# Making sixteen low weight halves on TensorE instead of VectorE, in an attention and two-layer-MLP kernel

## The chip, the cores and the metric

The kernel runs on one core of a Trainium2 chip, in one launch. The metric is the device time of that launch in microseconds (us). Before the change it is 1087.44 us, the median of three runs (1085.36 to 1089.29).

## The reference

Three layers follow each other, all in float32:

```
scores = q @ k^T / 8 + min(-(cum_i - cum_j), 0), causal      # cum = cumsum(max(s, 0))
x = softmax(scores) @ v                                      # 4 batches, 8 heads, 576 tokens, 64 wide
xn = x / rms(x) * rms_g                                      # 2304 tokens, 512 wide
x2 = (silu(xn @ w_gate) * (xn @ w_val)) @ w_out              # inner width 1536
out = (h - tanh(h)) @ w_out2,   h = x2 @ w_in                # inner width 2048
```

All weights arrive as float64 words. The kernel turns them into float32 and then into pairs of float16: a high half `hi = fp16(w * scale)` and a low half `lo = fp16(w * scale - hi)`. A product is three float16 matmuls (`mm3`, L675 to L678: high by high, high by low, low by high).

## The kernel before, in words

The work is tiled into 20 attention tiles of up to 128 query tokens (five to a batch) and six MLP blocks of 384 tokens. A block of the first MLP (`moe1_groups`: twelve `up1_g`/`up1_v` pairs, four `down1`) can start when its three or four attention tiles have been normalised (`emit_norm`, L513 to L531: ScalarE writes the high half of x, VectorE the low half at L529, two DMAs transpose them). A generator gives out the attention work in small steps, and the main program interleaves these with weight tasks and with MLP groups. The first block is interleaved with the preparation of the weights, the later ones with attention alone. A scheduler then sets each engine's own instruction order when the program is built; on the chip each engine works through its list in that order.

The weights of the first MLP are 24 pieces of 128 x 512 (`w1_tasks`): for j = 0, 1, 2 four gate pieces and four value pieces. A piece goes through these steps:

- a DMA brings its raw words into a part of tile `WO` (`raw_slots(WO, 2 * (n % 6))`, six places that are used in turn, issued at L540);
- VectorE decodes them in three instructions into float32 (L542 to L544, `w<-wo`), in `W1[:, n + 1, :]`;
- ScalarE squares the piece (L573) and TensorE adds up the squares (L589, `mm<-wo,rg`); a place for raw words is free again after that;
- after four pieces VectorE works out the scale (L593, L119 to L123, L596), a column of 128 numbers for each piece, `gsg` or `gsv`;
- `conv` calls `split`: ScalarE writes the high half (L558), VectorE the low half (L559), both into `W1[:, n, :]`. That is the place where the float32 of piece n - 1 lay, so the high half of a piece waits until the piece before has been read for the last time.

The weights of `w_out` (L559 `wo<-wo,tau`) and of the second MLP go through the same `split`. The names in the profile: `w` is the weight tile, `wo` the raw words or tile `WO`, `mm` a PSUM bank of the MLP, `st` the scores, `pv` the product with v, `sm` one of two PSUM banks (pool `ps_sm`) that the row maxima and small sums take in turn, `r` the row maxima, `tm`, `sh` and `sl` the MLP's inner values, `xth` and `xtl` the normalised x. In batch 0 the attention's product with v is in float32 (L477, 120 matmuls in the program, each of which the profile shows as two, with a weight load each), in the later batches in float16 (L479 to L481).

Of the kernel before, what the change touches and what calls it, by code (L numbers as in the profile page):

```python
# [7 lines left out]
FP32 = mybir.dt.float32  # L8
FP16 = mybir.dt.float16
# [31 lines left out]
def tile_forget_attention_moe_moe2(ctx, tc, qa, qb, kt, va, vb, va0, vb0, s, wg, wv, wo, rg, win, wo2, out):  # L41
# [28 lines left out]
    V, A, G, P, SY = nc.vector, nc.scalar, nc.gpsimd, nc.tensor, nc.sync  # L70

    ident = const.tile([128, 128], FP16, name="ident")
    bigid = const.tile([128, 128], FP16, name="bigid")
    maskn = const.tile([128, 128], FP16, name="maskn")
    ones_f = const.tile([128, 128], FP32, name="ones_f")
# [59 lines left out]
    def emit_consts():  # L135
        V.memset(lnp, LN_P)
        A.activation(out=warm, in_=lnp, func=ACTF.Exp)
        V.memset(halves, 0.0)
        for r in range(2):
            V.memset(halves[64 * r:64 * r + 64, r:r + 1], 1.0)  # L140
        V.memset(ident, 1.0)
        V.memset(bigid, 65504.0)
        V.memset(maskn, 0.0)
        V.memset(ones_f, 1.0)
        V.memset(ones_b, 1.0)
        V.memset(pat, 1.0)
        V.memset(pat[0:2], 0.0)
        G.affine_select(out=ident, in_=ident, pattern=[[1, 128]], compare_op=ALU.is_equal, fill=0.0, base=0, channel_multiplier=-1)
        G.affine_select(out=bigid, in_=bigid, pattern=[[1, 128]], compare_op=ALU.is_equal, fill=0.0, base=0, channel_multiplier=-1)
        G.affine_select(out=maskn, in_=maskn, pattern=[[-1, 128]], compare_op=ALU.is_ge, fill=-65504.0, base=0, channel_multiplier=1)  # L150
        for i in range(2):
            kc_consts(i)
        G.memset(tri, 0.0)
        G.affine_select(out=tri[:, 384:512], in_=tri[:, 384:512], pattern=[[-1, 128]], compare_op=ALU.is_ge, fill=-1e30, base=0, channel_multiplier=1)
        G.memset(spare(KC[2], 0)[0:64].bitcast(FP32), 0.0)
        for i in range(2):
            G.memset(QC[i][0:64].bitcast(FP32), 0.0)
        for i in range(2):
            G.memset(VT[i][64:128, 16:20, :].bitcast(FP32), 0.0)
# [396 lines left out]
    def split(W, n, sc):  # L556
        src, hi, lo = slot_f(W, n), slot_h(W, n), slot_l(W, n)
        A.activation(out=hi, in_=src, func=ACTF.Copy, scale=sc)  # L558
        V.scalar_tensor_tensor(out=lo, in0=src, scalar=sc, in1=hi, op0=ALU.mult, op1=ALU.subtract)  # L559

    def raw_tile(p, bufs):
        return p.tile([128, 512, 2], I32, name="raw", tag="raw", bufs=bufs)

# [14 lines left out]
    def w1_tasks(p):  # L578
# [24 lines left out]
                G.tensor_scalar(out=sig_s[j], in0=tl[j, "sg"], scalar1=sg, scalar2=2.0 ** -24, op0=ALU.mult, op1=ALU.mult)  # L603

        def conv(key, j, n, k):
            split(W1, n, tl[key, j, "s"][:, k:k + 1])

        for j in range(3):
            for key, src in (("g", wg), ("v", wv)):
# [584 lines left out]
```

## Time and profile before

| | us |
|---|---|
| median of three runs | 1087.44 |
| the profiled execution | 1086.19 |
| its span in the profile | 1084.4 |
| TensorE (PE) busy | 993.0 (92%) |
| VectorE (DVE) busy | 621.8 (57%) |
| ScalarE (ACT) busy | 604.1 (56%) |
| GpSimd (POOL) busy | 281.9 (26%) |

The profile's page divides the span into 40 slices. In the first eight (some 217 us) DVE is at 90% or more in most, while PE's slices lie between 10% and 90%; after them PE is at 90% or more nearly everywhere. Shares over the whole span therefore say little here: the stretch from 40 to 220 us is where weights are prepared beside attention, and it has to be read by itself.

### The profile page before, as it was taken

What the parts mean: (1) busy time and instruction counts of PE and PEld (TensorE: products, weight loads), DVE (VectorE), ACT (ScalarE), POOL (GpSimd) and SP (SyncE); (2) the same over time, 40 slices, a digit from 0 to 9 for tenths busy, and PEclk for the clock granted to TensorE, in tenths of its full rate; (3) what the DMA queues carried; (4) which work ended last, traced back from release to release, by engine and by line L of the source; (5) the groups of instructions that cost most, each with busy time, mean ns of one, the idle gap of its engine ahead of it and who ended that gap; (6) DMA issues with size and microseconds to landing.
All of it is one profiled execution on the core that took longest, in us unless ns stands there. A gap on an engine that the chain in (4) does not pass through costs nothing.

```text
span 1084.4 us, 19355 instructions
## 1 busy us (share of the span) xinstructions
PE 993.0 (92%) x7576; PEld 631.0 (58%) x7576; DVE 621.8 (57%) x1421; ACT 604.1 (56%) x1176; POOL 281.9 (26%) x377
## 2 busy tenths in 40 slices
PE   1488878899889999899999899999999999999998
PEld 1377545465556666556566556666666666666665
DVE  8987998966573540674543878485341605234250
ACT  6587668785854662767566447365342515243240
POOL 5122356424652450745345102100000000000000
PEclk9976989899999999999999999999999999999999
DMA  8714333330101212110100960141010010100000
GB/s 268 271 36 110 143 108 113 97 118 21 40 22 50 59 21 82 32 26 22 47 19 11 329 205 1 52 163 45 15 37 24 1 51 8 44 15 8 23 1 30
DMA packets 47517, 75.04 MB, mean 69 GB/s; under 512 B 25506, under 2 KB 33282, under 8 KB 46914
## 3 DMA queue, kind: packets, MB, share of 16 engines
q1 hardware_dynamic: 47426, 73.81, 21.5%
q8 instruction: 59, 0.97, 0.4%
q14 instruction: 32, 0.26, 0.1%
HBM read 59.42 MB, written 9.55 MB: 64 GB/s over the span
## 4 chain that ended last, share of the span: by engine, by line
PE 70%; DVE 15%; ACT 4%; DMA 4%; issue 4%; POOL 3%; SPq 0%; ACTq 0%; DVEq 0%; POOLq 0%
PE m L676 13%; PE m L678 13%; PE m L677 13%; PE mm L676 7%; PE mm L678 7%; PE mm L677 7%; PE pv L477 2%; PE st L435 1%; DVE w L559 1%; PE st L436 1%; POOL phl L457 1%; DVE w L543 1%; DVE q L351 1%; DMA w<-wo 1%; PE pv L479 1%
## 5 line engine op out<-in xcount | busy, mean ns | idle before, releaser
L676 PE MATMUL mm<-xth,w 128*128 128x384 f16 x480 | 160.9, 335 | 15.3 <-DVE tm L694 8.3
L678 PE MATMUL mm<-xth,w 128*128 128x384 f16 x480 | 159.9, 334 | 1.2 <-DVE w L559 1.2
L677 PE MATMUL mm<-xtl,w 128*128 128x384 f16 x480 | 160.7, 335 | 0.0
L1109 DVE SCALAR_TENSOR_TENSOR t<-m,u,t 128x384 f32<-128x384 f32 x96 | 59.2, 616 | 140.3 <-ACT t L1108 138.0
L677 PEld LDWEIGHTS <-w 128*128 128x128 f16 x960 | 95.0, 99 | 76.2 <-issue 22.8
L678 PEld LDWEIGHTS <-w 128*128 128x128 f16 x960 | 94.8, 99 | 65.2 <-issue 3.5
L676 PEld LDWEIGHTS <-w 128*128 128x128 f16 x960 | 95.8, 100 | 59.9 <-issue 4.4
L678 PE MATMUL m<-x2h,wi 128*128 128x384 f16 x384 | 125.2, 326 | 0.0
L677 PE MATMUL m<-x2l,wi 128*128 128x384 f16 x384 | 125.2, 326 | 0.0
L676 PE MATMUL m<-x2h,wi 128*128 128x384 f16 x384 | 125.2, 326 | 0.0
L678 PE MATMUL m<-dh,w 128*128 128x384 f16 x384 | 125.2, 326 | 0.0
L677 PE MATMUL m<-dl,w 128*128 128x384 f16 x384 | 125.2, 326 | 0.0
L676 PE MATMUL m<-dh,w 128*128 128x384 f16 x384 | 125.2, 326 | 0.0
L457 POOL TENSOR_TENSOR phl<-pf,phl 128x512 f16<-128x512 f32 (+2 forms) x90 | 96.0, 1073 | 46.6 <-ACT phl L450 45.7
L1116 POOL TENSOR_SCALAR io<-iso,isd 128x1 f32<-128x1 f32 x24 | 6.5, 271 | 375.8 <-ACT t L1122 314.4
L705 POOL TENSOR_TENSOR sl<-tm,sh 128x384 f16<-128x384 f32 x72 | 75.0, 1042 | 103.9 <-ACT sh L704 102.2
L445 POOL TENSOR_SCALAR_AFFINE_SELECT pf<-pf 128x128 f32<-128x128 f32 (+3 forms) x105 | 46.5, 445 | 187.2 <-ACT pf L443 186.8
L1110 ACT ACTIVATE dh<-t,sd 128x384 f16<-128x384 f32 x96 | 59.0, 615 | 60.9 <-DVE t L1109 60.7
L1122 ACT ACTIVATE t<-m,io 128x384 f32<-128x384 f32 x24 | 13.9, 580 | 141.0 <-PE m L678 141.0
L1111 DVE SCALAR_TENSOR_TENSOR dl<-t,sd,dh 128x384 f16<-128x384 f32 x96 | 59.2, 616 | 52.7 <-ACT dh L1110 51.9
L443 ACT ACTIVATE pf<-st,lnp,ilam 128x512 f32<-128x512 f32 (+2 forms) x105 | 73.1, 701 | 28.6 <-PE st L436 22.7
L676 PE MATMUL mm<-sh,wo 128*128 128x384 f16 x240 | 77.9, 326 | 1.8 <-DVE tm L694 1.8
(312 smaller groups left out, 2298.8 us busy)
## 6 DMA issues: line engine op xcount, KB each, us to landing
raw<-wo SPq DMA_DIRECT2D x16, 512.0 KB
w<-win SPq DMA_DIRECT2D x16, 512.0 KB
wo<-wg SPq DMA_DIRECT2D x12, 512.0 KB
wo<-wv SPq DMA_DIRECT2D x12, 512.0 KB
stk<-kt SPq DMA_DIRECT2D x4, 1152.0 KB
x2d<-tm SPq DMA_DIRECT2D x24, 192.0 KB
x2f<-x2d SPq DMA_DIRECT2D x6, 768.0 KB
out<-t SPq DMA_DIRECT2D x24, 192.0 KB
```

The lines of the kernel that those rows point to most:

```text
L443: A.activation(out=pf[:, 0:o], in_=ps[:, 0:o], func=ACTF.Exp, scale=bstate[b]["ilam"][:, hh:hh + 1], bias=lnp)
L445: G.affine_select(out=dg, in_=dg, pattern=[[0, len(heads)], [1, w]], compare_op=ALU.is_ge, fill=0.0, base=0, channel_multiplier=-1)
L457: G.tensor_tensor(out=u["pl"][:, 0:n], in0=u["pf"][:, 0:n], in1=u["ph"][:, 0:n], op=ALU.subtract)
L477: P.matmul(out=ps[0:w, o:o + 65], lhsT=u["pf"][:, cs], rhs=vs.bitcast(FP32), start=(c == 0), stop=(c == nch - 1))
L676: P.matmul(out=ps, lhsT=wh, rhs=xh, start=first, stop=False)
L677: P.matmul(out=ps, lhsT=wh, rhs=xl, start=False, stop=False)
L678: P.matmul(out=ps, lhsT=wl, rhs=xh, start=False, stop=last)
L705: moe_pend.append(lambda: G.tensor_tensor(out=SH["l"][:, f, :], in0=t, in1=SH["h"][:, f, :], op=ALU.subtract))
L1109: V.scalar_tensor_tensor(out=t, in0=ps, scalar=u[:, f // 4:f // 4 + 1], in1=t, op0=ALU.mult, op1=ALU.subtract)
L1110: A.activation(out=DH[:, f, :], in_=t, func=ACTF.Copy, scale=sd)
L1111: moe_pend.append(lambda: V.scalar_tensor_tensor(out=DL[:, f, :], in0=t, scalar=sd, in1=DH[:, f, :], op0=ALU.mult, op1=ALU.subtract))
L1122: A.activation(out=t, in_=ps, func=ACTF.Copy, scale=io)
```

## The change

For the pieces with j = 0 and 1, sixteen in all, `conv` calls a new function `split_pe`. It makes the low half by two matmuls into one `sm` bank: the float32 piece times a float32 diagonal of its scales, minus the high half through a float16 diagonal of -1. ScalarE makes the diagonal (128 x 128, from the identity) and brings the difference from PSUM to float16. The eight pieces of j = 2, and all other weights, stay with `split`. The diagonals lie in slot 12 of `WO`, one place for each k.

```diff
+    negid = const.tile([128, 128], FP16, name="negid")
...
+        V.memset(negid, -1.0)
...
+        G.affine_select(out=negid, in_=negid, pattern=[[1, 128]], compare_op=ALU.is_equal, fill=0.0, base=0, channel_multiplier=-1)
...
+    def split_pe(W, n, sc, i):
+
+        src, hi, lo = slot_f(W, n), slot_h(W, n), slot_l(W, n)
+        dg = WO[:, 12, 256 * i:256 * i + 256].bitcast(FP32)
+        A.activation(out=dg, in_=ident, func=ACTF.Copy, scale=sc)
+        A.activation(out=hi, in_=src, func=ACTF.Copy, scale=sc)
+        ps = sm_tile()
+        P.matmul(out=ps, lhsT=dg, rhs=src, start=True, stop=False)
+        P.matmul(out=ps, lhsT=negid, rhs=hi, start=False, stop=True)
+        A.activation(out=lo, in_=ps, func=ACTF.Copy)
+
...
         def conv(key, j, n, k):
-            split(W1, n, tl[key, j, "s"][:, k:k + 1])
+            if j < 2:
+                split_pe(W1, n, tl[key, j, "s"][:, k:k + 1], k)
+            else:
+                split(W1, n, tl[key, j, "s"][:, k:k + 1])
```

The scheduler orders every engine anew. Lines of the changed kernel are three higher than before from L151 to L560 (L529 becomes L532, L400 becomes L403, L542 becomes L545) and up to seventeen higher after (L676 becomes L693, L593 becomes L607, L589 becomes L603).

VectorE just ahead of the low half of tile 1's x (the second L529) before the change; `qke` to `qks` is the chain of batch 1's scales:

```order
L119 TENSOR_SCALAR qke<-sm 128x4
L120 TENSOR_SCALAR qke<-qke 128x4
L121 TENSOR_SCALAR qke<-qke 128x4
L123 RECIPROCAL qks<-qke 128x4
L246 TENSOR_SCALAR cap<-qke,sig_c 128x2
L593 TENSOR_REDUCE nmv_800<-mm 128x1
L247 TENSOR_TENSOR qks<-qks,cap 128x2
L386 TENSOR_REDUCE r8b<-sm 128x4
L529 SCALAR_TENSOR_TENSOR xl<-x,ss,xh 128x512
```

The same place after the change, up to the first step of the value pieces' scale:

```order
L545 TENSOR_SCALAR w_117<-wo 128x512 x2
L530 SCALAR_TENSOR_TENSOR ss<-ss 128x1
L546 SCALAR_TENSOR_TENSOR w_117<-wo,w_117 128x512 x2
L547 SCALAR_TENSOR_TENSOR w_117<-wo,w_117 128x512 x2
L245 TENSOR_SCALAR ssqk<-halves,ssqk 128x2
L532 SCALAR_TENSOR_TENSOR xl<-x,ss,xh 128x512
L499 SCALAR_TENSOR_TENSOR rr<-pv,vone 128x4
L500 RECIPROCAL rr<-rr 128x4
L607 TENSOR_REDUCE nmv_819<-mm 128x1
```

The normalisation of tile 1 now stands ahead of batch 1's scales and of tile 4's row maxima (L386); 20 rows earlier in VectorE's list (row 154, was 174), and that of tile 2 in row 179 (was 210).

TensorE where the first MLP block begins, after the change (L571 and L572 are the two new matmuls; L693 to L695 are `mm3`):

```order
L693 MATMUL mm<-xth,w_117 128x384
L694 LDWEIGHTS w_117
L694 MATMUL mm<-xtl,w_117 128x384
L695 LDWEIGHTS w_117
L695 MATMUL mm<-xth,w_117 128x384
L572 LDWEIGHTS negid
L572 MATMUL sm<-w_117,negid 128x512
L693 LDWEIGHTS w_117
L693 MATMUL mm<-xth,w_117 128x384
L571 MATMUL sm<-w_117,wo 128x512
L694 LDWEIGHTS w_117
L694 MATMUL mm<-xtl,w_117 128x384
```

The new matmuls stand between those of the MLP. In TensorE's list the first `mm3` matmul follows 58 of batch 0's 120 products with v where it followed 76, and seven L571 stand ahead of it; the twelfth `mm3` matmul follows eight L571. The last L571 stands ahead of the last ten of those 120.

ScalarE at the first gate pieces, before (`gsg` is the scale column):

```order
L416 ACTIVATE rt<-sm 16x128
L558 ACTIVATE w_116<-w_116,gsg_544 128x512 x2
L443 ACTIVATE pf<-st,lnp,ilam 128x512
L443 ACTIVATE phl<-st,lnp,ilam 128x512
L558 ACTIVATE w_116<-w_116,gsg_544 128x512 x2
L573 ACTIVATE wo<-w_116 128x512
L443 ACTIVATE pf<-st,lnp,ilam 128x512
```

And after (L568 makes a diagonal, L569 the high half):

```order
L419 ACTIVATE rt<-sm 16x128
L568 ACTIVATE wo<-ident,gsg_547 128x128
L569 ACTIVATE w_117<-w_117,gsg_547 128x512
L568 ACTIVATE wo<-ident,gsg_547 128x128 x3
L446 ACTIVATE pf<-st,lnp,ilam 128x512
L446 ACTIVATE phl<-st,lnp,ilam 128x512
L587 ACTIVATE wo<-w_117 128x512
```

Three of the four high halves have gone to later places, behind the exponentials of tile 1, and four diagonals have come in.

## Rows read from the trace of the kernel before

**Rows 1.** Busy time by stretch (us, instructions), TensorE's granted clock (1.00 is full), DMA.
```profile
core 0: us, PE busy (x) PEld busy (x) DVE busy (x) ACT busy (x) POOL busy (x), PEclk, DMA share, GB/s
40.00:100.00 60.00, 50.22 (x377) 42.18 (x376) 54.16 (x142) 45.85 (x92) 14.31 (x27) 0.75 0.33 88
100.00:160.00 60.00, 49.31 (x415) 30.89 (x413) 53.51 (x117) 38.35 (x82) 22.33 (x26) 0.87 0.39 122
160.00:220.00 60.00, 50.87 (x489) 32.29 (x488) 57.03 (x152) 46.88 (x104) 34.65 (x42) 0.90 0.34 104
220.00:240.00 20.00, 20.00 (x147) 12.38 (x146) 13.30 (x35) 17.13 (x37) 3.86 (x7) 1.00 0.47 142
```

**Rows 2.** The chain of waits, 40 to 160 us: shares, then pieces (start, us).
```profile
by line: PE pv L477 19.7%; DVE w L559 7.1%; issue 6.0%; DVE w L543 5.1%; DVE r L400 4.9%; DVE w L542 3.9%; DMA wo<-wv 3.7%; DVE w L544 3.7%; DMA wo<-wg 3.3%; DVE xl L529 2.7%; DVE kl L276 2.2%; PE st L435 2.2%; PE st L436 2.1%; PE mm L676 1
...
88.66 8.73 PE pv L477 x40
```

**Rows 3.** Busy time in 4 us stretches around 88 us, columns as in rows 1.
```profile
84.00:88.00 4.00, 0.77 (x11) 0.47 (x8) 4.00 (x12) 3.96 (x10) 2.74 (x3) 0.81 1.29 252
...
92.00:96.00 4.00, 4.00 (x21) 4.00 (x20) 3.22 (x12) 3.93 (x7) 1.36 (x3) 0.50 0.07 15
```

**Rows 4.** Timeline of TensorE: start, us, [idle before].
```profile
49.23 1.06 PE L477 MATMUL pv<-vt,pf 128*128 128x65 f32 x8
50.12 1.09 PE L477 MATMUL pv<-vt,phl 128*128 128x65 f32 x8
...
88.39 0.27 PE L414 MATMUL sm<-ident,r 128*8 128x128 f16 x1 [3.40 <-DVE r L411]
88.59 1.97 PE L477 MATMUL pv<-vt,pf 128*128 128x65 f32 x8
90.35 1.91 PE L477 MATMUL pv<-vt,phl 128*128 128x65 f32 x8
...
103.93 0.51 PE L676 MATMUL mm<-xth,w 128*128 128x384 f16 x1
104.23 1.91 PE L589 MATMUL mm<-wo,rg 128*128 128x512 bf16 x4
105.94 0.52 PE L677 MATMUL mm<-xtl,w 128*128 128x384 f16 x1
...
123.48 0.80 PE L477 MATMUL pv<-vt,phl 128*64 128x65 f32 x10
124.21 0.20 PE L435 MATMUL st<-q,kl 128*128 128x64 f16 x1
```

**Rows 5.** Groups of instructions, 40 to 160 us: count, busy us, mean ns, idle before.
```profile
L559 DVE SCALAR_TENSOR_TENSOR w<-w,gsg 128x512 f16<-128x512 f32 x8 | 8.6, 1070 | 0.0
L559 DVE SCALAR_TENSOR_TENSOR w<-w,gsv 128x512 f16<-128x512 f32 x7 | 5.2, 740 | 0.9 <-ACT w L558 0.9
L499 ACT ACTIVATE x<-pv,rr 128x64 f32<-128x64 f32 x32 | 7.3, 321 | 0.8 <-DVE xl L529 0.8
L443 ACT ACTIVATE pf<-st,lnp,ilam 128x512 f32<-128x512 f32 x7 | 5.4, 768 | 0.0
L573 ACT ACTIVATE wo<-w 128x512 bf16<-128x512 f32 x21 | 12.9, 624 | 1.8 <-DVE w L544 1.7
L558 ACT ACTIVATE w<-w,gsg 128x512 f16<-128x512 f32 x8 | 5.8, 720 | 4.3 <-DVE w L559 3.8 <-DVE gsg L596 0.5
```

**Rows 6.** Timeline of VectorE: start, us.
```profile
88.70 2.61 DVE L276 SCALAR_TENSOR_TENSOR kl<-stk,qks,kl 64x2304 f16<-64x2304 f32 x1
...
99.25 0.75 DVE L529 SCALAR_TENSOR_TENSOR xl<-x,ss,xh 128x512 f16<-128x512 f32 x1
...
160.66 1.51 DVE L559 SCALAR_TENSOR_TENSOR w<-w,gsv 128x512 f16<-128x512 f32 x1
```

**Rows 7.** Groups of GpSimd in the first 40 us, columns as in rows 5.
```profile
L877 POOL TENSOR_SCALAR rg<-ones_f,rgs 128x128 bf16<-128x128 f32 x4 | 2.7, 678 | 7.2 <-DMA rgs<-rg 7.2
L149 POOL TENSOR_SCALAR_AFFINE_SELECT bigid<-bigid 128x128 f16<-128x128 f16 x1 | 0.3, 285 | 0.0
```

## Prediction

> **What bounds the kernel now.** I read the page's slices first, then busy time by stretch, then the chain of waits for the first stretches, then the timelines of PE and DVE at the places it names. By stretch [rows 1], PE is full from 220 us on (20.00 of 20, and nearly so in the page's later slices), so what is gained or lost before that goes through to the end nearly whole. From 40 to 220 us three engines share the load: DVE is busy 54.16 + 53.51 + 57.03 = 164.7 of 180 us (92%), PE 150.4 (84%), ACT 131.1 (73%). DVE is the tightest. PE is not as loose as its idle time says, because it does not run at full clock: 0.75, 0.87 and 0.90. With levels of 1.2 and 2.4 GHz a mean of 0.75 is half the time at the lower one; the time at the lower level is 2 x (1 - clock) x 60, that is 30, 15.6 and 12 us, and half of each (28.8 us) would be saved at full clock. PE's idle time is 9.8, 10.7 and 9.1 us. So PE has 29.6 us of idle time and 28.8 us of slow clock to take up new work in, if the work falls there.
>
> The chain from 40 to 160 us [rows 2] has both engines: 19.7% are batch 0's float32 products with v on PE, 7.1% (8.5 us of 120) the low halves L559, more than any other DVE line. The worst PE piece is 8.73 us from 88.66. There [rows 3, 4] PE had been idle 3.40 us for DVE's row maxima, and from 88 us on it is busy without a gap at a granted clock of 0.50 until the MLP's matmuls begin at 103.93. These wait for tile 2's low half on DVE at 99.25 [rows 6], which stands behind a low half of k (2.61 us) and the low halves of the gate and value pieces.
>
> **The change, part by part.**
>
> *DVE loses* sixteen L559: 8.6 + 5.2 + 1.51 (the sixteenth, at 160.66) = 15.3 us [rows 5, 6], 9% of its work in the stretch. The chain holds 8.5 us of them up to 160 us; the last counts too, since DVE is busy 57.03 of 60 us there: 10 us together. What is late next on DVE is the decoding, which the new order moves ahead.
>
> *PE gains* sixteen pairs of matmuls. No row has a float32 matmul of 512 columns. Those of 65 columns show as two records each. Eight records with 128 weight columns take 50.12 - 49.23 = 0.89 us, and 90.35 - 88.59 = 1.76 us at the lower clock (twice as much, so the first were at the upper one); ten with 64 weight columns take 124.21 - 123.48 = 0.73 us [rows 4]. The record of 0.111 us so falls to 0.073 with half the weights, and PEld is busy 4.00 of 4 us in such a run [rows 3]: the short ones go by their weight loads, and the long ones have no more weights to load. From above: scaled by columns, 2 x 512/65 x 0.111 = 1.75 us by the first row, 1.15 by the second. From below: two passes at the float16 rate. That rate is L589's, four in 105.94 - 104.23 = 1.71 us at the lower clock [rows 4], 0.43 each and 0.21 at the upper, so 0.43 us. I take 0.8, between 0.43 and 1.15, the two rows that weight loads distort least; with the second matmul, like L589, a pair is 1.01 us at the upper clock (0.64 to 1.96) and 2.02 at the lower. By the order, eight pairs stand about where the 40 to 100 us stretch was, half at each level: 8 x 1.5 = 12.0. The other eight are in the next stretch, with 26% at the lower level: 8 x 1.27 = 10.2. I take 22.2 us (16.2 at the upper clock alone, 32.3 at the lower).
>
> The Trainium skill (FP8 and Floating Point Precision, "TensorE Precision Notes") has true float32 as four passes through the array; by that an estimate is 4 x 0.21 = 0.86 us, and the sum would be 1.3 us higher. No row here shows the passes.
>
> *ACT gains* sixteen diagonals and sixteen copies from PSUM; the high halves stay. A diagonal lies between 0.32 (128 x 64) and 0.72 (128 x 512, also with a scale column) [rows 5], nearer the first: 0.38. The copy lies between 0.62 (a square, no scale column) and 0.77 (the exponential out of PSUM, two columns) [rows 5]: 0.64. Together 16.3 us (15.0 to 23.8), nearly all from 40 to 160 us, where ACT idles 14.2 + 21.7 = 35.9 us [rows 1]. I count it at nothing, with that idle time as cover; it is a rival below.
>
> *Waits added.* The second matmul waits for the high half, and attention and MLP matmuls stand behind it on PE. The copy waits for both matmuls, and exponentials stand behind it on ACT. The high half of the next piece now waits for PE where it waited for DVE (3.8 us in eight) [rows 5]. Each pair also holds one of the two `sm` banks for about 0.8 to 1.6 + 0.2 to 0.4 + 0.64 us, so the row maxima have one bank meanwhile. Between nothing and 1 us a piece; I take nothing, since the new order puts other work between hi and the pair in most places, and keep 16 us in the range.
>
> *Set-up.* One memset on DVE and one selection (0.285 us) on GpSimd, which waits 7.2 us for a DMA right behind it [rows 7]: nothing.
>
> *What moves.* The new lists put tile 1's and tile 2's normalisation ahead on DVE, by 20 and 31 rows, past batch 1's scales, one of k's low halves of 2.61 us [rows 6] and seven L559. On PE the MLP then starts after 58 instead of 76 products with v, and its float16 matmuls come between the rest. SP's loads of raw words follow L589 as before; DMA is busy 0.33 to 0.39 of its time [rows 1].
>
> *The clock.* In before, PE runs products with v, 20 of them without a break, busy and at 0.50, from 88.6 to 105.9 us [rows 2 to 4]: 17.3 us that would be 8.65 at full clock. At 49 us the same products ran at the upper clock, behind float16 matmuls [rows 4]. With the idle 3.40 us filled and MLP matmuls between them I expect the upper level: -8.6 us.
>
> The Trainium skill (TensorE: Matmul & The Clock Gate, "Part 1: The HAM clock gate") says that the array is throttled by default and that sustained matmul activity releases the throttle. The trace does not agree for the short float32 matmuls: PE is busy 4.00 of 4 us and stays at 0.50 [rows 3]. If the rule held for the long ones, sixteen pairs would cost 16.2 us and the sum would be 6 us lower (rival 4).
>
> *Sum.* Added on PE 22.2. Taken back: 10 by DVE's shorter chain, 8.6 by the clock, and of PE's idle time from 40 to 160 us, 20.5 less the 8.5 of the chain already counted, three quarters filled by the new pairs, 9. Net -5.4 us on the profiled execution's 1086.2 (span 1084.4 and 1.8 around it): 1080.8. The median of the runs is 1.25 above that execution: 1082.
>
> **The rivals.**
>
> 1. *Slower: PE pays in the slow clock.* The mechanism is that float32 matmuls do not raise the clock, and sixteen long ones among 120 short ones keep it down. Place: 50 to 105 us. Price: the first eight pairs at 2.02 (16.2) and eight at 1.27 (10.2) make 26.4, with no clock gain: 26.4 - 10 - 9 = +7.4, 1094.8; with all pairs at the lower clock 32.3 - 19 = +13.3, 1100.7. It decides if the granted clock from 40 to 100 us stays at 0.75 or falls: without the 8.6 us the sum is already +3.2. For it: the 17 us at 0.50 with PE busy. Against it: that run is bound by weight loads, which the long ones are not. Chance 0.22.
>
> 2. *Slower: ACT becomes the bound.* ACT works in order; each copy may hold it until the pair is done, about 1.2 + 0.3 - 0.72 = 0.8 us for a piece. 84.2 busy + 16.3 + 12.8 is 113 of 120 us, and DVE's 10 us would be gone: 1092. For it: ACT at 3.96 of 4 us at 84 us [rows 3]. Against it: three high halves moved to later places. Chance 0.11.
>
> 3. *No change.* Half of the clock gain missed (4.3) makes -1.1, 1086.3; a third of the idle time as well (3) +1.9, 1089.3. The case is 1084.2 to 1090.7. Chance 0.20.
>
> 4. *Faster by more*: all pairs at the upper clock (16.2), -11.4, 1076. It is the far end of the forecast's case.
>
> **How the numbers follow.** The forecast's case, faster, has 0.47, with a range of its own from 1072 to 1084.2. 0.3% is about what a measurement of this kernel tells from no change, so the bounds are 1084.2 and 1090.7. Faster 0.47, same 0.20, slower 0.22 + 0.11 = 0.33. The range runs from 1070 (1076 with another 5.3 us, DVE's whole 15.3 gained) to 1102 (all of rival 1; the float32 matmul at its upper bound of 1.75 us, by the same mix 20 us more, less part of it in idle time; or 2 with 10 of the 16 us of waits): some 0.06 lies below it and 0.10 above.
>
> **What would show it.** Right: the first `mm3` matmul before 97 us; a granted clock of 0.85 or more from 40 to 100 us; most of the sixteen L571 (two records each) below 1.2 us together; DVE's share in that stretch below 85%. Wrong: pairs at 2 us with the clock near 0.7 (rival 1); PE idle behind ACT's high halves, or ACT idle behind L572 by more than 8 us in all (rival 2); the last `w_out` low half not earlier. The forecast fails if the weights are ready earlier and the end still is not, which would say that PE's added work, not DVE's chain, sets the end.

## The result, and the profile after

The changed kernel takes 1091.9 us (median of 16 runs, 1088.1 to 1099.0), the kernel before 1086.5 in as many runs beside it. The ratio is 1.0051, with a 95% interval of 1.0037 to 1.0066: slower by half a per cent, 5.4 us, where 1082 had been forecast. The profiled execution has a span of 1090.4 us at a mean granted clock of 0.980, against 1084.4 at 0.970.

Busy time of the changed kernel by stretch, columns as in [rows 1]:

```profile
40.00:100.00 60.00, 49.26 (x325) 35.67 (x324) 40.86 (x115) 45.26 (x99) 11.19 (x23) 0.83 0.31 91
100.00:160.00 60.00, 53.39 (x432) 34.08 (x432) 55.24 (x127) 48.23 (x103) 21.84 (x26) 0.97 0.41 131
160.00:220.00 60.00, 49.07 (x505) 31.36 (x504) 55.88 (x137) 45.24 (x97) 31.30 (x41) 0.97 0.32 100
220.00:240.00 20.00, 17.39 (x115) 10.30 (x113) 12.98 (x33) 11.84 (x25) 2.88 (x5) 0.83 0.16 41
```

Against [rows 1], the granted clock rose from 0.75, 0.87 and 0.90 to 0.83, 0.97 and 0.97, as forecast. DVE fell from 54.16 to 40.86 us in the first stretch. But TensorE is busy 49.26 + 53.39 + 49.07 + 17.39 = 169.1 us of the 200, where it was 170.4: its idle time is 30.9 us, not smaller than the 29.6 before. It fell from 20.5 to 17.4 us between 40 and 160 us, and rose from 9.1 to 13.5 between 160 and 240 us: in the last stretch, where TensorE had been full, it now has 2.6 us of idle time at a clock of 0.83. Over the whole span it hardly changed. The page of the changed kernel has

```profile
PE 1000.6 (92%) x7624; PEld 632.0 (58%) x7624; DVE 613.7 (56%) x1406; ACT 615.9 (56%) x1208; POOL 275.7 (25%) x378
```

so TensorE's idle time is 1090.4 - 1000.6 = 89.8 us, where it was 1084.4 - 993.0 = 91.4.

The new work, from the groups of the changed kernel from 40 to 240 us (columns as in [rows 5]; L571 is the float32 matmul, two records each, L572 the float16 one behind it, L568 the diagonal, L573 the copy):

```profile
L571 PE MATMUL sm<-w,wo 128*128 128x512 f32 x32 | 18.8, 670 | 0.2 <-DVE r L403 0.2
L573 ACT ACTIVATE w<-sm 128x512 f16<-128x512 f32 x16 | 9.4, 587 | 2.6 <-PE sm L572 2.6
L572 PE MATMUL sm<-w,negid 128*128 128x512 f16 x16 | 6.3, 395 | 0.0
L569 ACT ACTIVATE w<-w,gsv 128x512 f16<-128x512 f32 x8 | 5.7, 717 | 2.5 <-PE sm L571 2.5
L568 ACT ACTIVATE wo<-ident,gsg 128x128 f32<-128x128 f16 x8 | 2.7, 389 | 0.0
```

The timeline of TensorE (start, us, what) shows the pairs' price from start to start, which is safer than the modelled busy times; it answers to [rows 4]:

```profile
56.57 1.13 PE L571 MATMUL sm<-w,wo 128*128 128x512 f32 x2
57.54 0.38 PE L572 MATMUL sm<-w,negid 128*128 128x512 f16 x1
57.75 0.78 PE L480 MATMUL pv<-vt,phl 128*128 128x65 f32 x6
...
61.30 1.08 PE L571 MATMUL sm<-w,wo 128*128 128x512 f32 x2
62.21 0.38 PE L572 MATMUL sm<-w,negid 128*128 128x512 f16 x1
...
89.21 2.02 PE L571 MATMUL sm<-w,wo 128*128 128x512 f32 x2
91.16 0.64 PE L385 MATMUL sm<-kc,qc 128*64 128x512 f16 x2
...
95.95 1.74 PE L571 MATMUL sm<-w,wo 128*128 128x512 f32 x2
97.53 0.38 PE L572 MATMUL sm<-w,negid 128*128 128x512 f16 x1
97.74 1.02 PE L571 MATMUL sm<-w,wo 128*128 128x512 f32 x2
98.60 0.33 PE L693 MATMUL mm<-xth,w 128*128 128x384 f16 x1
98.76 1.03 PE L603 MATMUL mm<-wo,rg 128*128 128x512 bf16 x4
```

At the upper clock a pair is 0.86 to 0.97 us for the float32 matmul (97.74 to 98.60, 56.57 to 57.54) and 0.21 us for the float16 one (57.54 to 57.75); at the lower clock the float32 matmul is 1.95 us (89.21 to 91.16). Only two of the sixteen, at 89.21 and 95.95, met the lower clock. All together they come to 20.2 us, 18 of them at full clock. The first `mm3` matmul starts at 98.60, where it was 103.93.

VectorE waits where it had worked. These are its five longest waits from 40 to 110 us, as total, times and longest:

```profile
DVE nmg L607 <- PE mm L603: 5.9, 1, 5.9
DVE w L545 <- DMA wo<-wv: 4.2, 2, 2.3
DVE rr L499 <- PE pv L480: 3.7, 2, 2.1
DVE ss L525 <- ACT xl L241: 3.3, 3, 2.1
DVE w L545 <- DMA wo<-wg: 1.2, 1, 1.2
```

and three places of its timeline, in brackets the idle time before and what ended it (`...` marks lines left out):

```profile
93.23 0.69 DVE L389 TENSOR_REDUCE r<-sm 128x1 f32<-128x512 f32 x1
99.83 0.69 DVE L607 TENSOR_REDUCE nmg<-mm 128x1 f32<-128x512 f32 x1 [5.91 <-PE mm L603]
...
103.39 0.43 DVE L545 TENSOR_SCALAR w<-wo 128x512 int32<-128x512 int32 x1 [1.85 <-DMA wo<-wv]
...
244.59 0.75 DVE L562 SCALAR_TENSOR_TENSOR wo<-wo,tau 128x512 f16<-128x512 f32 x1 [0.74 <-ACT wo L561]
```

The row maximum of the squares at 99.83 stands behind 5.91 us of nothing: the squares' matmuls L603 run at 98.76, behind the pairs of 95.95 and 97.74 in the timeline above. These two take 2.7 us (95.95 to 98.60) of that wait; scores and products with v ahead of them, most of them at the lower clock, take the rest. The last low half of `w_out` starts at 244.59; before, it started at 239.95. TensorE did not wait for that one, but for the first, which starts at 222.43 where it had started at 215.00: TensorE is idle until 223.23 for it. So say its own waits from 40 to 240 us (total, times, longest): first the one for the row maxima before the change, then three in the changed kernel, of which the second is the one for the row maxima again and the third is for the reduction `won` over a part of `w_out`:

```profile
PE sm L414 <- DVE r L411: 4.7, 2, 3.4
```

```profile
PE mm L695 <- DVE wo L562: 2.6, 1, 2.6
PE sm L417 <- DVE r L414: 1.7, 1, 1.7
PE sm L395 <- DVE won L666: 2.2, 1, 2.2
```

The MLP starts earlier, but the attention falls behind: the last of batch 0's float32 products with v starts at 156.1 us, where it was 142.5 (L480, L477).

### The profile page after: what moved, and what is told of

It reads as the page before. It is cut to its first block, busy times and chain, and to the rows that moved or that the text cites. A ratio compares the mean times of both kernels' runs of the same rounds, so it can differ in the third digit from the quotient of the medians.

```text
span 1090.4 us, 19467 instructions
## 1 busy us (share of the span) xinstructions
PE 1000.6 (92%) x7624; PEld 632.0 (58%) x7624; DVE 613.7 (56%) x1406; ACT 615.9 (56%) x1208; POOL 275.7 (25%) x378
## 4 chain that ended last, share of the span: by engine, by line
PE 69%; DVE 14%; DMA 7%; ACT 4%; issue 3%; POOL 2%; SPq 1%; ACTq 0%; DVEq 0%; POOLq 0%
PE m L693 13%; PE m L695 13%; PE m L694 13%; PE mm L693 7%; PE mm L695 7%; PE mm L694 7%; DMA w<-wo 1%; PE st L439 1%; PE st L438 1%; POOL phl L460 1%; DMA wo<-wv 1%; DMA stv<-qb 1%; DVE w L546 1%; DVE w L547 1%; PE pv L480 1%
## 5 line engine op out<-in xcount | busy, mean ns | idle before, releaser
L693 PE MATMUL mm<-xth,w 128*128 128x384 f16 x480 | 158.4, 330 | 14.9 <-DVE tm L711 8.0
L694 PE MATMUL mm<-xtl,w 128*128 128x384 f16 x480 | 158.1, 329 | 0.0
L695 PE MATMUL mm<-xth,w 128*128 128x384 f16 x480 | 158.0, 329 | 0.0
L695 PEld LDWEIGHTS <-w 128*128 128x128 f16 x960 | 94.2, 98 | 63.2 <-issue 3.2
L693 PEld LDWEIGHTS <-w 128*128 128x128 f16 x960 | 95.2, 99 | 57.7 <-issue 3.6
L695 PE MATMUL m<-x2h,wi 128*128 128x384 f16 x384 | 125.2, 326 | 0.0
L693 PE MATMUL m<-x2h,wi 128*128 128x384 f16 x384 | 125.2, 326 | 0.0
L695 PE MATMUL m<-dh,w 128*128 128x384 f16 x384 | 125.2, 326 | 0.0
L693 PE MATMUL m<-dh,w 128*128 128x384 f16 x384 | 125.2, 326 | 0.0
L722 POOL TENSOR_TENSOR sl<-tm,sh 128x384 f16<-128x384 f32 x72 | 71.8, 998 | 120.9 <-ACT sh L721 119.1
L448 POOL TENSOR_SCALAR_AFFINE_SELECT pf<-pf 128x128 f32<-128x128 f32 (+3 forms) x105 | 42.6, 407 | 154.0 <-ACT pf L446 153.5
L695 PE MATMUL mm<-sh,wo 128*128 128x384 f16 x240 | 78.9, 329 | 2.6 <-DVE wo L562 2.6
```

The costliest lines, as they stand in the source:

```text
L448: G.affine_select(out=dg, in_=dg, pattern=[[0, len(heads)], [1, w]], compare_op=ALU.is_ge, fill=0.0, base=0, channel_multiplier=-1)
L693: P.matmul(out=ps, lhsT=wh, rhs=xh, start=first, stop=False)
L694: P.matmul(out=ps, lhsT=wh, rhs=xl, start=False, stop=False)
L695: P.matmul(out=ps, lhsT=wl, rhs=xh, start=False, stop=last)
L722: moe_pend.append(lambda: G.tensor_tensor(out=SH["l"][:, f, :], in0=t, in1=SH["h"][:, f, :], op=ALU.subtract))
```

## The experiments

**How the runs are compared.** Every run has a span and a mean granted clock. Span times clock is the time the same run would take if its time at the lower level counted half; I call it the time at full clock, and the rest, span x (1 - clock), the loss to the clock. It is a sum worked out from two readings, not a measured time; idle time at the lower level counts half in it too. Means over the runs of each kernel (times in us; the ratio is to runs of the kernel before beside them, with its 95% interval). The kernel before was run again beside each of the five sets of experiments: its mean span was 1084.1 to 1085.1, its time at full clock 1055.0 to 1056.7 and its loss 28.1 to 30.1, so differences of one or two us between rows of different sets (e, f, g, h, k) say nothing:

```
kernel            median   ratio to before           span   full clock   loss
before            1086.5   -                         1084.8   1056.1     28.7
after             1091.9   1.0051 [1.0037, 1.0066]   1090.4   1067.9     22.5
e1_relief         1100.9   1.0125 [1.0103, 1.0147]   1098.7   1057.6     41.1
e2_act            1090.7   1.0042 [1.0027, 1.0057]   1089.7   1054.6     35.1
e3_fp16           1088.5   1.0015 [1.0001, 1.0029]   1087.0   1060.4     26.6
e4_pe             1111.5   1.0233 [1.0207, 1.0258]   1110.3   1075.4     34.9
f2_old_in_new     1110.0   1.0222 [1.0201, 1.0243]   1108.4   1061.4     47.0
f3_fp16_in_new    1097.9   1.0113 [1.0080, 1.0146]   1096.5   1061.4     35.1
f4_relief_in_old  1081.8   0.9964 [0.9950, 0.9977]   1080.3   1055.3     25.1
f6_relief_in_new  1102.5   1.0152 [1.0134, 1.0171]   1100.8   1061.2     39.6
g1_new_in_old     1110.2   1.0199 [1.0172, 1.0226]   1107.0   1075.8     31.2
g2_bank           1101.3   1.0134 [1.0113, 1.0155]   1099.7   1069.5     30.2
g3_swap           1093.9   1.0068 [1.0047, 1.0088]   1092.5   1069.7     22.8
g4_half           1094.6   1.0077 [1.0056, 1.0099]   1093.3   1065.8     27.5
h1_buf_in_new     1091.1   1.0042 [1.0025, 1.0059]   1089.1   1067.1     22.0
h2_buf_in_old     1084.9   0.9990 [0.9977, 1.0003]   1083.9   1055.8     28.1
h3_buf_free       1101.1   1.0136 [1.0120, 1.0152]   1099.5   1054.4     45.1
k1_old_early      1090.1   1.0039 [1.0023, 1.0055]   1088.5   1051.5     37.0
k2_new_early      1094.6   1.0073 [1.0048, 1.0099]   1092.6   1069.3     23.3
k3_old_load       1090.0   1.0026 [1.0009, 1.0043]   1087.5   1054.3     33.2
```

### One part at a time, the order left to the scheduler

**e1_relief**: VectorE's relief alone.

```diff
     def split_pe(W, n, sc, i):
-        A.activation(out=dg, in_=ident, func=ACTF.Copy, scale=sc)
         A.activation(out=hi, in_=src, func=ACTF.Copy, scale=sc)
-        P.matmul(out=ps, lhsT=dg, rhs=src, start=True, stop=False)
-        P.matmul(out=ps, lhsT=negid, rhs=hi, start=False, stop=True)
-        A.activation(out=lo, in_=ps, func=ACTF.Copy)
+        V.tensor_scalar(out=lo, in0=hi, scalar1=2.0 ** -11, scalar2=None, op0=ALU.mult)
```

> DVE's relief by itself. For the first 16 pieces the low half is replaced by a short scaled copy of the high half on DVE (float16, 512 columns); nothing is added on TensorE or ScalarE. What is left out: the true low halves of these pieces. Theory A (the failed step is that DVE's shorter chain is worth nothing, since waits on TensorE, loads and the weights' own chain take its place): 1084 to 1089 us, no change from before. Theory B (DVE's relief is worth its 8 to 10 us, and TensorE's pairs cost more than 15): 1076 to 1079 us. Theory C (the change's time is that of the new order in which the scheduler puts everything): any time from 1080 to 1095, not tied to what is removed.

Measured: 1100.9 us. With less work than before on VectorE and no more on any other engine it is 14 us slower, so theories A and B are both off. It is above the range of C (the order) too; that the order is the cause is what f4 shows below, with the same work at 1081.8.

**e2_act**: ScalarE writes the low half straight from the piece.

```diff
-        P.matmul(out=ps, lhsT=dg, rhs=src, start=True, stop=False)
-        P.matmul(out=ps, lhsT=negid, rhs=hi, start=False, stop=True)
-        A.activation(out=lo, in_=ps, func=ACTF.Copy)
+        A.activation(out=lo, in_=src, func=ACTF.Copy, scale=dg[:, 0:1])
```

> The relief of DVE and the load of ScalarE without TensorE's pairs: the diagonal is still made, and the low half is written by ScalarE straight from the float32 piece with the scale. What is left out: the subtraction of the high half. Theory A: the waits on TensorE and its 16 pairs (18 us) are gone, ScalarE has room: 1084 to 1089 us, as with the relief alone. Theory B: 1078 to 1082 us. Rival (ScalarE is the bound, rival 2 of the prediction): 1090 us or more.

Measured: 1090.7 us, the lower edge of what the ScalarE rival wanted. At full clock it is 1054.6, no more than before: ScalarE's 17 us more of work are hidden, and the loss to the clock is 5 us above that of the runs beside it (30.1). Its order is its own, so that its time alone does not decide on the rival.

**e3_fp16**: cheap pairs.

```diff
-        P.matmul(out=ps, lhsT=dg, rhs=src, start=True, stop=False)
+        P.matmul(out=ps, lhsT=ident, rhs=hi, start=True, stop=False)
```

> The change with cheap pairs: the float32 matmul is replaced by a float16 one of the same shape (identity by the high half), so that a pair takes some 0.43 us instead of 1.15 at the upper clock; all waits, ScalarE's work and the banks stay. What is left out: the precision of the low half, which becomes zero. Theory A (TensorE's added time goes to the end): after less 16 x 0.72 = 11.5 us, 1079 to 1084 us. Rival (waits between TensorE and ScalarE, not TensorE's time): 1089 to 1092 us, as after.

Measured: 1088.5 us, 3.4 below after, a miss for theory A's 11.5 and just below the rival's range. At full clock 7.5 of the 11.5 us did go; the clock took 4.1 back.

**e4_pe**: the pairs alone, and nobody reads them (the diff is against the kernel before).

```diff
+        ps = sm_tile()
+        P.matmul(out=ps, lhsT=ones_f, rhs=src, start=True, stop=False)
+        P.matmul(out=ps, lhsT=negid, rhs=hi, start=False, stop=True)
         V.scalar_tensor_tensor(out=lo, in0=src, scalar=sc, in1=hi, op0=ALU.mult, op1=ALU.subtract)
```

> TensorE's pairs alone: before, with 16 dead pairs (float32 ones by the piece, and the negative identity by the high half, into a bank that nobody reads); DVE still makes every low half, and ScalarE has nothing more. Theory A (18 us of work, 10 of it back by the clock, none in idle time): 1092 to 1098 us. Theory B (DVE's relief is worth 10): 1098 to 1104 us, above after by these 10. If idle time took the pairs, as the prediction had it for 9 us: 1086 to 1090 us.

Measured: 1111.5 us, above every expectation. At full clock it is 1075.4, some 20 above before: the whole 18 us of the pairs are on the path, and TensorE's idle time took none of them in this order. In the profiled execution it is 1108.8 - 1010.8 = 98.0 us, where it was 91.4.

### The order held

An edit moves rows in all engines' lists, and e1 suggests that this alone can cost 14 us. So the next kernels keep one kernel's order: an order edge from each instruction to the next on its engine, without a wait.

```diff
...
+    for n in zlib.decompress(base64.b85decode(ROWS)).decode().split():
+        i = at["I-" + n]
+        if i.engine in prev:
+            tc.add_manual_dep(i, prev[i.engine].name, ...)
+        prev[i.engine] = i
```

`ROWS` are the names of the instructions in the order that is kept. The edges by themselves cost nothing that shows: h1 and h2 below, each in its own order with one small edit, are within 2 us of after and before.

**f2_old_in_new**: the kernel before (each low half by the diff's old line), in the order of the changed kernel.

> The old work in the new order: the kernel before, with every instruction of every engine held in the order of the changed kernel by order edges; each low half stands on DVE where the second matmul of its pair stood on TensorE; no pairs, diagonals or copies. Theory W (TensorE's added work is what makes the change slower, the new order is neutral or better): after less 18 us of pairs, plus 5 to 12 us for the low halves on DVE, 1079 to 1086 us. Theory O (the new order itself is worse, the pairs are hidden in it): 1088 to 1096 us.

**f6_relief_in_new**: as f2, with e1's short copy as low half.

> DVE's relief in the new order: as f2, with the short copy on DVE in place of the true low half (left out). Against f2 it gives what DVE's low halves cost in the new order, against the changed kernel what pairs, diagonals and copies cost. Theory A: within 3 us of f2. Theory B: 8 to 12 us below f2. If the pairs' 18 us go to the end whole: 1073 to 1076 us; if half: 1082 us.

**f3_fp16_in_new**: e3's diff, in the order of the changed kernel.

> The cheap pairs of e3 once more, now with every instruction held in the order of the changed kernel, so that nothing differs from it but the time of 16 matmuls (float16 in place of float32, low halves zero). Theory W (TensorE's time goes to the end whole): 16 x 0.72 = 11.5 us below after, 1080 to 1083 us. Theory O: 1089 to 1092 us. Between the two: that part of the pairs' time which the order hides.

Measured: f2 1110.0, f6 1102.5, f3 1097.9, after 1091.9 us. f2 and f3 lie above the ranges of both theories; f6 is 7.5 below f2, just short of B's 8, but by the clock alone (at full clock 1061.2 and 1061.4). Less work on TensorE makes the kernel slower here, by 6 us (f3) and by 10.6 (f6). In a fixed order that can't come from the time of the work; the clock shows where it comes from. (f3's runs spread from 1092.1 to 1106.7, so its 6 us are rough. Its low halves are zero; f2, in the same order with the true ones, loses 47.0 us, so the zeros are not what lowers the clock.) Busy time of f6 by stretch and of f3 in the first one, columns as in [rows 1]:

```profile
40.00:100.00 60.00, 47.41 (x300) 38.45 (x297) 41.97 (x120) 38.86 (x84) 12.06 (x22) 0.67 0.29 89
100.00:160.00 60.00, 46.90 (x406) 31.04 (x407) 52.95 (x121) 41.46 (x81) 20.82 (x24) 0.90 0.41 131
```

```profile
40.00:100.00 60.00, 49.47 (x289) 39.20 (x288) 39.70 (x112) 40.35 (x91) 11.23 (x21) 0.68 0.29 86
```

The first stretch is at 0.67 and 0.68, where the changed kernel has 0.83; the second is at 0.90 in both, where it has 0.97. In stretches of 4 us, first f6 and then the changed kernel:

```profile
60.00:64.00 4.00, 4.00 (x25) 3.44 (x25) 1.76 (x8) 2.86 (x6) 0.00 (x0) 0.50 0.15 34
...
76.00:80.00 4.00, 4.00 (x20) 3.72 (x21) 2.00 (x9) 1.84 (x4) 0.59 (x2) 0.50 0.00 0
```

```profile
60.00:64.00 4.00, 3.67 (x30) 2.45 (x30) 2.76 (x10) 3.95 (x9) 0.29 (x1) 1.00 0.15 34
...
76.00:80.00 4.00, 2.22 (x22) 1.91 (x21) 4.00 (x13) 3.49 (x5) 1.91 (x2) 1.00 0.02 6
80.00:84.00 4.00, 2.51 (x9) 1.75 (x10) 1.94 (x6) 3.47 (x13) 0.29 (x1) 0.53 0.35 70
```

f6 is at 0.50 in every stretch from 68 to 104 us, even with TensorE busy 4.00 of 4 us at 76 us. The changed kernel, in the same order and with pairs at 56.57, 61.30, 63.70 and 68.26, is at 1.00 in every stretch from 60 to 80 us and loses the clock there, behind a stretch with 2.22 of 4 us busy. In the table f6 loses 39.6 us to the clock and the changed kernel 22.5: pairs, diagonals and copies together come with 17 us less of loss in the changed kernel's order and cost 6.7 at full clock. f3, which has all of them but float16 matmuls in place of the float32 ones, loses 35.1: the float32 matmuls by themselves come with 12.6 us less of loss, and cost 6.5 at full clock.

**f4_relief_in_old**: e1's short copy as low half, in the order of the kernel before.

> DVE's relief in the old order: the kernel before, every instruction held in its own order, and the first 16 low halves replaced by the short float16 copy of e1 (about 12 us less on DVE; what is left out is the true low half). This is e1 without e1's new order. Theory A (DVE's relief is worth nothing, because DVE is not what sets the pace): 1084 to 1088 us. Theory B (it is worth the 8 to 10 us that the prediction counted): 1076 to 1079 us. If e1's 1101 us came from the relief and not from its order: about 1100 us.

Measured: 1081.8 us, 4.4 below the kernel before in the runs beside it (3.8 in the mean spans), between A and B. At full clock it is 0.7 below (1056.0 beside it); the loss to the clock is 3.0 below (28.1). e1, with the same work, is at 1100.9: its 19 us more came from its order. The 10.5 us that are off VectorE (15.3 less sixteen copies of 0.30) were not on the path as the chain had them.

**g1_new_in_old**: the change with all shared instructions in the order of the kernel before, except the first 16 high halves.

```diff
-        ps = sm_tile()
         P.matmul(out=ps, lhsT=dg, rhs=src, start=True, stop=False)
...
-                split_pe(W1, n, tl[key, j, "s"][:, k:k + 1], k)
+                split_pe(W1, n, tl[key, j, "s"][:, k:k + 1], k, tl[key, j, "ps"])
```

> The change in the old order: every instruction that both kernels have is held in the order of the kernel before on its engine; only the first 16 high halves, the diagonals, the pairs and the copies are placed by the scheduler between them. The pairs use the bank in which the squares of the same four pieces were summed, not one of the two small banks, since the old order leaves those no place. Theory O (what makes the change slower is the new order, and the pairs pay for themselves by the clock and by idle time): before less DVE's 4.4 us of f4, with pairs that cost between 0 and 5 us net: 1081 to 1087 us. Theory W (18 us of pairs, 10 to 12 back by the clock, whatever the order): 1088 to 1094 us. If the old order's waits for the pairs are long: above 1095 us.

Measured: 1110.2 us. That is the third expectation, and theory O falls as it stood: the new order is not bad as such, since the new work in the old order is as slow as the old work in the new one (f2). At full clock each order fits best the work that it was made for: g1 is 6.3 us above g2 below, which has the same bank in an order of its own, and f2 5.3 above before. The longest of TensorE's waits from 40 to 245 us (total, times, longest) shows a part: the pairs wait for the copies that empty their one bank, 7.9 us.

```profile
PE mm L570 <- ACT w L572: 7.9, 6, 2.3
```

### Other orders for the same work

**g2_bank**: g1's bank, the order left to the scheduler.

> The change with the pairs in the bank of the squares, free for the scheduler to order: another order for the same work. Theory O: any time from 1080 to 1105 us, by the order alone, with TensorE's full-clock work (span less idle and slow clock) within 3 us of after's 983. Theory W: 1089 to 1094 us, as after, since the work is the same.

**g3_swap**: two lines of ScalarE change places in the text.

```diff
-        A.activation(out=dg, in_=ident, func=ACTF.Copy, scale=sc)
         A.activation(out=hi, in_=src, func=ACTF.Copy, scale=sc)
+        A.activation(out=dg, in_=ident, func=ACTF.Copy, scale=sc)
```

> The change with one neutral edit: the high half is written down ahead of the diagonal, not behind it; both are on ScalarE. Work, banks and waits are the same, the scheduler's order differs from after's in some hundred rows early in the program. Theory W: within 2 us of after. Theory O: off by more than 3 us, either way, if the early rows move.

**g4_half**: `if j < 1` for `if j < 2`, eight pieces.

> The change for the first eight pieces alone (j = 0). Theory W: the price goes by pieces, half of after's 5.4 us: 1088 to 1090 us. Theory O: the order differs from both kernels, so that the time is not between the two, below 1085 or above 1093 us.

Measured: 1101.3, 1093.9 and 1094.6 us. g3 is 2.0 above after, at the edge of W's range and short of O's. g2 is outside W's range and inside O's. Half the change (g4) is slower than all of it, as O had it. At full clock the three agree with the work: 1069.5 and 1069.7 for sixteen pieces (after 1067.9), 1065.8 for eight. g2 is not a matter of order alone: its pairs share one bank for four pieces, and g1 has shown what that costs in waits.

**h1_buf_in_new, h2_buf_in_old, h3_buf_free**: the squares go to free rows of `W1`, so that the load of a piece's raw words no longer waits for the matmul that sums the squares of the piece six before it. h1 is the changed kernel in its own order, h2 the kernel before in its own, h3 the kernel before with the order left to the scheduler.

```diff
-        sq = junk16(raw)
+        sq = W[:, 18 + n % 6, 0:512].bitcast(BF16) if n < 12 else junk16(raw)
```

> Raw loads that do not wait for TensorE: the changed kernel, every instruction held in its own order, but the squares of the first twelve pieces go to free rows of W1 instead of the buffer of raw words, so that the load of the raw words six pieces on no longer waits for the matmul that sums the squares (which stands behind pairs on TensorE). The result is the same. Theory L (TensorE's idle time from 40 to 110 us comes from the weights' own chain: squares behind pairs, loads behind squares, so that DVE's relief is lost there): 3 to 8 us below after, 1084 to 1089, with idle time of TensorE below 87 us. Theory P (the idle time is many short waits for DVE, ScalarE and GpSimd, of which each one taken away uncovers the next): within 2 us of after, 1090 to 1094.

> The same edit in the kernel before, held in its own order. Theory L has the late loads as a result of the pairs: here no change, 1085 to 1088 us. If the loads are late in both kernels: 1080 to 1084 us. Theory P: 1085 to 1088 us.

> The edit of h2 with the order left to the scheduler: another order for the work of the kernel before. If an order made for the same work differs by more than 3 us from h2, the spread of orders is as large as the change's result (Theory O): anywhere from 1078 to 1100 us. Otherwise within 2 us of h2.

Measured: 1091.1, 1084.9 and 1101.1 us. In h1 the wait did shrink. VectorE's five longest waits from 40 to 110 us, as above:

```profile
DVE nmg L607 <- PE mm L603: 5.9, 1, 5.9
DVE rr L499 <- PE pv L480: 5.3, 2, 3.7
DVE r L403 <- PE sm L402: 2.5, 6, 0.9
DVE ss L525 <- ACT xl L241: 2.0, 1, 2.0
DVE w L545 <- DMA wo<-wv: 1.7, 1, 1.7
```

Its waits for raw words fell from 5.4 to 1.7 us; that for PV rose, and one for the row maxima (L403) came up. TensorE's busy time and clock from 40 to 240 us, first the changed kernel, then h1:

```profile
40.00:240.00 200.00, 169.11 (x1372) 111.41 (x1371) 164.96 (x409) 150.57 (x321) 67.21 (x93) 0.91 0.33 100
```

```profile
40.00:240.00 200.00, 172.72 (x1367) 112.70 (x1367) 164.31 (x410) 150.35 (x320) 67.05 (x93) 0.90 0.33 100
```

Its idle time fell by 3.6 us (169.11 to 172.72 busy of 200), and the clock from 0.91 to 0.90, which is 2 us of it: the end stays within some 1 us. Over the span its idle time is 86.1 us (1090.7 - 1004.6), below the 87 that theory L named, and the end did not follow: L falls as a cause of the result. Theory P's time holds; that each wait taken away uncovers the next is seen here for one wait. h2 is no change. h3, the work of the kernel before in another order, is 14.6 us slower than before, by the table all of it clock (45.1 us lost against 28.7, and 1054.4 at full clock against 1056.1). Of that the stretches to 220 us hold some 4 us (0.76, 0.84 and 0.86 against the 0.75, 0.87 and 0.90 of [rows 1]); the rest lies behind them. The second and third:

```profile
100.00:160.00 60.00, 53.14 (x423) 37.26 (x425) 43.98 (x105) 40.54 (x87) 18.86 (x24) 0.84 0.33 79
160.00:220.00 60.00, 49.22 (x455) 30.28 (x456) 56.76 (x122) 40.22 (x90) 32.37 (x38) 0.86 0.36 109
```

**k1_old_early, k2_new_early, k3_old_load**: three more orders.

```diff
-        with tc.issue_after(last_r[0]) if left[0] < 8 else ExitStack():
+        with tc.issue_after(last_r[0]) if left[0] < 10 else ExitStack():
```

in the kernel before (k1) and in the changed one (k2), and for k3 in the kernel before

```diff
-                if i == nu - 1 and T + 2 < 20 and T > 0:
+                if i == nu - 2 and T + 2 < 20 and T > 0:
```

> Another order for the work of the kernel before: the weight tasks that may stand only behind the third tile's maxima on PE are the last ten of the first 16 instead of the last eight; no work is added or removed. Theory O (the spread of orders is as large as the change's result): more than 3 us off before, as h3. If before's order is an ordinary one: as often below 1086 as above it. TensorE's full-clock work 963 to 968 us in either case.

> The same edit in the changed kernel: another order for the work of the change. Theory O: more than 3 us off after, either way. If the change's work as such is what costs, this stays above k1 by about 5 us. TensorE's full-clock work 981 to 985 us.

> A third order for the work of the kernel before: each later tile's queries are loaded one unit earlier in the program. No work is added or removed. Theory O: more than 3 us off before, above it, since before's order would then be a lucky one among orders; otherwise within 3 us of 1086.

Measured: 1090.1, 1094.6 and 1090.0 us; k2 is 4.5 above k1, as expected if the change's work as such costs; it is 2.7 above after, short of theory O's 3. k1 and k3 are some 3.5 above before (k1's interval is 2.5 to 6.0); k3's interval, 1.0 to 4.7 us, does not settle whether it is more than the 3 us of its theory O. Over four orders of the scheduler for each kind of work (old: before, h3, k1, k3; new: after, g2, g3, k2) the time at full clock is 1051.5 to 1056.1 and 1067.9 to 1069.7, the loss 28.7 to 45.1 and 22.5 to 30.2. The two kinds do not overlap at full clock, whatever the order; in span they do, 1084.8 to 1099.5 and 1090.4 to 1099.7. The means of the four are 1054.1 and 1069.1 at full clock, 36.0 and 24.7 of loss: over these orders the change costs 15.0 us at full clock and gets 11.3 back by the clock.

All three other orders of the old work are slower than the kernel before. k3's expectation had a name for that: before's order is a lucky one among orders, and a part of what an edit costs here can be that it gives up this order. No run shows how large that part is in the 5.4 us.

No version with the whole work beats the kernel before; h2 can't be told from it.

## Why the prediction was wrong

The direction was wrong. In the two readings of the table the result is +11.8 at full clock and -6.2 by the clock, +5.6 us of span. Against the prediction's terms: the pairs cost 2 us less than its 22.2, the clock gave about what it had (6.2 us, after 2 us that two pairs lost at the lower level), and some 13 of the 19 us that were to come back from idle time and VectorE's chain did not.

- **TensorE's 22.2 us: right within 10%.** 20.2 in the trace. At the upper clock a pair is 1.14 us (0.93 + 0.21) where 1.01 was taken, 18 us for 16.2; and 2 instead of about 6 us more at the lower clock, since 14 pairs, not 8 or 10, met the upper one.
- **The clock's 8.6 us: near in size, by another mechanism than the one told.** From 40 to 160 us the loss fell from 0.25 x 60 + 0.13 x 60 = 22.8 us [rows 1] to 0.17 x 60 + 0.03 x 60 = 12.0, by 10.8; over the whole span and all runs it fell by 6.2. The prediction expected this from filled idle time and from MLP matmuls between the short products. The idle time of the first stretch was not filled (10.7 us, before 9.8), and f3 and f6, with the same MLP matmuls in the same order, stand at 0.68 and 0.67 in it and at 0.90 in the second, where the changed kernel has 0.83 and 0.97 and the kernel before 0.75 and 0.87. So it is the long float32 matmuls that do most of it, which the prediction had only in rival 4 (all pairs at the upper clock); that its figure came out near is luck. Rival 1 had the mechanism the wrong way round, though its 1094.8 is 2.9 us from the measured time.
- **The step that failed: the 10 us for VectorE's chain and the 9 us of idle time, as two sums that add up.** Both had to come out of TensorE's idle time, 8.5 and 9 of its 20.5 us from 40 to 160 us alone. It fell there by 3.1, to 17.4, rose again by 4.4 from 160 to 240 us, and over the two profiled executions it fell by 1.6 (91.4 to 89.8). By the means of the table the end got 18 - 11.8, about 6 of the 19 us; over four orders of each kind, 18 - 15.0, about 3. f4 has VectorE's relief by itself at 4.4 us, 0.7 of them at full clock; e4 has idle time taking none of the pairs. I read 8.5 us of the chain of waits [rows 2] as time that would go, and named the decoding as what is late next without a price. What was late next on VectorE: the squares' matmuls behind the pairs (5.9 us of its waiting), the raw words (5.4), PV (3.7). In f6, the same order without pairs, they are 1.3, 5.8 and 2.6 us, so the first comes with the pairs and the raw words are late without them too. With the raw words taken away, in h1, others took their place and the end did not move. On TensorE the wait for the row maxima went from 4.7 to 1.7 us, and 2.6 us for the first low half of `w_out` and 2.2 us for its reduction `won` came in.
- **ScalarE's 16.3 us at nothing: right.** The diagonal is 0.389, the copy 0.587 us, and ScalarE waited 2.6 us for L572 and 2.5 for L571, where rival 2 asked for more than 8; e2 has its work hidden at full clock. Rival 2 is out, though its 1092 is the figure nearest to the measured 1091.9: that is luck.
- **What moves, taken at nothing: wrong by more than the result.** The order alone moves the old work by some 3.5 to 14.6 us, in all three cases up from before. The prediction had looked at where the lists moved, but gave the new list no range of its own.
- **Its own signs.** First `mm3` 98.60 (97 was asked for), clock 0.83 (0.85), 14 of the 16 L571 below 1.2 us (yes), VectorE's share 68% (below 85%, yes), the last low half 4.6 us later (no). The last line of the prediction, weights ready earlier and the end not, is in part what happened: the MLP started 5.3 us earlier while the attention fell behind, and the weights of `w_out` came later, the first low half by 7.4 us, the last by 4.6; TensorE waited 2.6 us for the first.

The float32 matmul is 0.86 to 0.97 us at the upper clock, start to start. The Trainium skill (FP8 and Floating Point Precision, "TensorE Precision Notes") has true float32 as four passes; the prediction's estimate by them, 0.86 us, agrees. The clock of the same order is 0.83 with the long float32 matmuls and 0.67 or 0.68 without them, and f6 is busy 4.00 of 4 us at 76 us, mostly with the short float32 ones, and stays at 0.50. The rule of the Trainium skill (TensorE: Matmul & The Clock Gate, "Part 1: The HAM clock gate"), that the throttled state is the default and sustained matmul activity releases the throttle, agrees with the long float32 matmuls and does not agree with the short ones.

What stays open: why one order of the same instructions keeps the clock at 0.97 and another at 0.96 over the span, and which row decides it. So it is open how much of the 5.4 us is the price of the change and how much that of leaving before's order. Four orders each give 3.7 us between the means of the spans (1090.1 and 1093.8), 1.7 without g2 (1091.8); both are less than the spread of either.

## What to carry to other kernels

Idle time of the bound engine that consists of many short waits took up little new work here (91.4 us before, 89.8 after). Count work that is added to such an engine at its whole price at the upper clock unless a run shows otherwise, and price what is taken off another engine by a held-order run, not by that engine's share of the chain. Where a scheduler orders the program, an edit makes a new program: run two or three neutral variants of each side before a difference of one per cent is put down to the edit. Split each time into span times clock and the loss to the clock: over the scheduler's orders here the first followed the work within 2 to 5 us, and the second moved with the order by up to 16.

## What the runs showed of the hardware that was not expected

- Sixteen long float32 matmuls, 18 us of work, came with 12.6 us less of loss to the clock than float16 ones in the same places and order (35.1 and 22.5), and with 17 us less than the same order without pairs, diagonals and copies (39.6).
- Taking work away from TensorE can cost time: float16 in place of float32 in the same order made the kernel some 6 us slower (1097.9 against 1091.9).
- The same work has a loss to the clock anywhere from 28.7 to 45.1 us in four orders.
